# Mask tables from an earlier n, and a softmax normalisation shared by VectorE and GpSimd

## The chip, the cores and the metric

The kernel runs on one core of a Trainium2 chip. The metric is the device time of one execution in microseconds (us). A core has five engines that each run their own list of instructions in order: TensorE (PE, matmuls; its weight loads are listed as PEld), VectorE (DVE), ScalarE (ACT), GpSimd (POOL) and SyncE (SP, which here only issues DMA transfers). An instruction waits on semaphores until what it needs is there, and everything behind it on the same engine waits with it.

## The reference

```python
# q, k, v: (2, 8, 768, 64); n_global = 8, n_local = 96; two MLP layers 512 -> 2048 -> 512
rel = pos[:, None] - pos[None, :]
is_global = pos[None, :] < n_global
is_local = (rel >= 0) & (rel < n_local)
dist = np.where(is_global & ~is_local, n_local, np.abs(rel))
scores = q @ k.T / sqrt(D) - slope[h] * dist          # slope[h] = 2 ** (-8 (h + 1) / H)
scores = np.where(is_global | is_local, scores, -1e9)
a = np.exp(scores - max(scores));  a = a / (sum(a) + 1e-9)
x = (a @ v)            # heads side by side: 1536 tokens x 512
h = x @ w_in;  x = (h * sigmoid(h)) @ w_out           # first layer
h = x @ w2_in; out = np.maximum(0.01 * h, h) @ w2_out  # second layer
```

`n_global` and `n_local` are inputs: they are 64-bit integers that the kernel reads from memory, so the mask is computed on the chip.

## The kernel before

Attention is cut into 24 units (2 batches, 3 blocks of 256 query rows, 4 pairs of heads). Unit n goes through these steps: its q and k arrive by DMA; PE transposes them into the PSUM tile `pt` (L936); ACT or DVE copies them out as `kT` and ACT as `qT`, and DVE repeats the first 32 keys in `kT` (L948); PE computes the scores `s` (L979); DVE adds the mask and takes the row extreme (`nm`, L1012); ACT takes the exponential and its row sum (L1019); DVE makes the reciprocal `rs` of the sums (L1025, L1026) and multiplies the four quarters of the tile `A` by it (L1035, "the normalisation": two row blocks i, two heads j; 256 columns wide, or 128 in the first row block of a sequence); PE transposes `A` into `pa` (L1052, once for each row block, as soon as that block's two quarters are normalised); ACT or DVE copies it to `AT`; PE multiplies by v into `pv` (L1078); ACT and DVE split that into a high and a low part in `x`. There are two buffers of `A`.

The MLP follows: weights arrive as 64-bit numbers in `st`, and ACT and DVE make two 32-bit parts of them (L273 to L288); PE does `ph` and `pq` (first product), `po` (second product). MLP work on PE, DVE and ACT fills the gaps of the attention as far as its inputs are there.

No order is written by hand. `Sched` is a list scheduler that runs while the program is built: every task has engines it may run on, a cost for each, a priority and what it depends on; the scheduler walks through its own modelled time and gives each idle engine the ready task of best priority. What comes out is a fixed list of instructions for each engine. A task with several engines goes to whichever is idle first. Dummy matmuls on zeros (`wps`, L878: 8 at the start, then a few, then 16 as fillers of low priority) keep PE running before there is real work.

At the start q of unit 0, then `n_global` and `n_local`, then q of unit 1 go out on SP's queue, and k of units 0 and 1 on ACT's. The mask (L828 to L844) is made by nine small DVE instructions and two POOL instructions after the two numbers have landed. `mask` serves a full block, `mask0` the first one of a sequence.

DMA transfers of SP and ACT take eight semaphores in turn: the ninth one issued waits until the first has landed.

Of the kernel before, what the change touches and what calls it, by code (L numbers as in the profile page):

```python
# [26 lines left out]
def kernel(  # L27
# [49 lines left out]
    def load_n(eng):  # L77
        for x, src in enumerate((n_global, n_local)):
            eng.dma_start(out=nraw[:, x], in_=src.bitcast(I32).partition_broadcast(P))
# [5 lines left out]
    m8nl = const.tile([P, 1], F32, name="m8nl")  # L85

# [33 lines left out]
    class Sched:  # L120
# [19 lines left out]
        def run(self):  # L140
# [3 lines left out]
            for t in self.tasks:  # L144
                for e in t["eng"]:
                    free.setdefault(e, 0.0)
                    ready.setdefault(e, [])
                for b in t["bufs"]:
                    if b.tile is not None and not b.held:
                        b.held = True  # L150
                        used[b.key] = used.get(b.key, 0) + 1
            seq, dma = 0, 0.0
# [12 lines left out]
            while len(order) < len(self.tasks):  # L165
                for e in free:
# [22 lines left out]
                    if t["dma"]:  # L189
                        dma = max(dma, now + 0.4) + t["land"]  # L190
                        end = max(end, dma) + 1.7
                    else:
                        end += t["land"]
# [591 lines left out]
    with ExitStack() as es:  # L785
# [28 lines left out]
        m8rel, pen, col = mk[:, 0:256], mk[:, 256:512], mk[:, 512:640]  # L814
        nc.gpsimd.iota(
            m8rel[:, P:256], pattern=[[8, P]], base=0, channel_multiplier=-8, allow_small_or_imprecise_dtypes=True
        )
        nc.gpsimd.affine_select(
# [5 lines left out]
        )  # L824
        nc.gpsimd.iota(col, pattern=[[1, P]], base=0, channel_multiplier=0, allow_small_or_imprecise_dtypes=True)

        def masks_n():
            nc.vector.tensor_copy(npair, nraw)  # L828
            nc.vector.tensor_scalar(nhi, npair[:, :, 0], 0.0, None, op0=ALU.is_lt)
            nc.vector.tensor_tensor(nhi, nhi, npair[:, :, 1], op=ALU.add)  # L830
            nc.vector.scalar_tensor_tensor(nf, nhi, float(2.0 ** 32), npair[:, :, 0], op0=ALU.mult, op1=ALU.add)
            nc.vector.tensor_scalar(m8nl, nlf, -8.0, None, op0=ALU.mult)

        def masks_global(eng):
            eng.tensor_scalar(col, col, ngf, -BIG, op0=ALU.is_ge, op1=ALU.mult)
            eng.tensor_scalar(col, col, m8nl, 0.0, op0=ALU.add, op1=ALU.add)

        def masks_local():
            nc.vector.tensor_scalar(pen, m8rel, m8nl, -BIG, op0=ALU.is_le, op1=ALU.mult)
            nc.vector.tensor_tensor(mask, m8rel, pen, op=ALU.add)  # L840

        def masks_both():
            nc.vector.tensor_copy(mask[:, NPV:P], col[:, 0:NG])
            nc.vector.tensor_tensor(mask0, mask[:, P:256], col, op=ALU.max)  # L844

        masks = (masks_n, masks_global, masks_local, masks_both)
# [13 lines left out]
        nload = add("SP", 0.9, lambda eng: load_n(eng), -13.0, (), (), land=0.1)  # L860
        add("ACT", 1.4, lambda eng: eng.activation(warm, warm, AF.Exp), -9.0, (), (), at=2.0)
        mt = add("DVE", 0.95, lambda eng: masks[0](), -0.5, (nload,), (), at=3.9)
        mp = add("POOL", 0.9, lambda eng: masks[1](eng), -0.5, (mt,), ())
        mt = add("DVE", 0.75, lambda eng: masks[2](), -0.5, (mt,), ())
        mtask = add("DVE", 0.45, lambda eng: masks[3](), -0.5, (mt, mp), ())
# [133 lines left out]
        def st_P(u):  # L999
# [30 lines left out]
            for i in range(2):  # L1030
                c0 = P if 2 * sb + i == 0 else 0
                for j in range(2):
                    def norm(eng, i=i, j=j, c0=c0):
                        a = A()[:, i, j, c0:256]
                        eng.tensor_scalar(a, a, rs()[:, 2 * i + j:2 * i + j + 1], None, op0=ALU.mult)  # L1035

                    u["norm"].append(add("DVE", 0.26, norm, n + 0.3, (rt,), (A, rs)))
# [228 lines left out]
```

## Time and profile before

| | |
|---|---|
| time, median of 3 runs | 606.26 us (606.16 to 608.05) |
| time of the profiled execution | 607.96 us |
| span of its instructions | 606.2 us |
| PE busy | 596.1 us (98%) |
| DVE busy | 528.4 us (87%) |
| ACT busy | 305.4 us (50%) |
| POOL busy | 3.7 us (1%) |
| chain that ended last | PE 94%, DVE 3%, DMA 2%, ACT 1% |

The span counts from the first to the last instruction of the trace; 1.8 us lie around it. Busy shares are averages over stages with different limits, so the stages have to be looked at one by one: the start (no input yet), the first units of attention, attention beside the MLP, and the MLP alone.

### The profile page before, as it was taken

To read this page: it belongs to the slowest core of one execution; us is meant where nothing else is said; L and a number is where in the kernel's file an instruction comes from. 1 tells how busy PE (TensorE), PEld (TensorE's weight loads), DVE (VectorE), ACT (ScalarE), POOL (GpSimd) and SP (SyncE) were. 2 spreads that over 40 slices of the span, in tenths; PEclk is the share of its full clock that TensorE was granted. 3 is DMA by queue.
4 is the path that set the end of the run, shared out by engine and by line. 5 is a ranking of instruction groups with operands and counts; after the bars stand their busy time and mean duration, and the time that the engine had idled before them with its cause. 6 is when DMAs were issued, how large, how long until landed. Compare 5 with 4: busy or idle time off the path is not lost.

```text
span 606.2 us, 9115 instructions
## 1 busy us (share of the span) xinstructions
PE 596.1 (98%) x3266; PEld 490.0 (81%) x3267; DVE 528.4 (87%) x1213; ACT 305.4 (50%) x682; POOL 3.7 (1%) x20
## 2 busy tenths in 40 slices
PE   8999999999999999999999999999999999999996
PEld 4678777778888888888888888898898889888985
DVE  4999999877999999995999999899999997978551
ACT  4789887876654435432555554556343433333110
POOL 2000000000000000000000000000000000000000
PEclk9999999999999999999999999999999999999999
DMA  8875568310012332322231111322132322010112
GB/s 180 185 174 141 136 167 203 71 36 1 0 36 70 105 105 69 106 69 70 69 105 35 36 35 36 105 69 85 54 105 71 104 70 69 6 65 1 70 55 90
DMA packets 72676, 49.43 MB, mean 82 GB/s; under 512 B 50480, under 2 KB 67120, under 8 KB 72624
## 3 DMA queue, kind: packets, MB, share of 16 engines
q1 hardware_dynamic: 71536, 48.51, 28.6%
q8 instruction: 28, 0.46, 0.3%
q10 hardware_dynamic: 1088, 0.26, 0.2%
q14 instruction: 24, 0.20, 0.1%
HBM read 45.62 MB, written 3.15 MB: 80 GB/s over the span
## 4 chain that ended last, share of the span: by engine, by line
PE 94%; DVE 3%; DMA 2%; ACT 1%; issue 0%; ACTq 0%
PE po L655 43%; PE pq L490 29%; PE ph L600 10%; PE s L979 3%; PE pa L1052 3%; PE pv L1078 3%; PE pt L936 2%; DMA st<-in_moe_w_in_dram 1%; DVE A L1012 1%; PE wps L878 1%; DMA q<-in_q_dram 1%; DVE A L1035 0%; DMA k<-in_k_dram 0%; ACT AT L222 0%; ACT A L1019 0%; DVE f L279 0%
## 5 line engine op out<-in xcount | busy, mean ns | idle before, releaser
L655 PE MATMUL po<-g,wo 128*128 128x512 f32 x576 | 141.5, 392 | 0.0
L655 PE MATMUL po<-wo,g 128*128 128x512 f32 (+1 forms) x588 | 136.2, 385 | 0.0
L655 PEld LDWEIGHTS po<-wo,g 128*128 128x128 f32 x588 | 107.7, 188 | 21.0
L655 PEld LDWEIGHTS po<-g,wo 128*128 128x128 f32 x576 | 106.9, 188 | 21.7 <-DVE wo L288 0.2
L600 PE MATMUL ph<-x,wi 128*128 128x512 f32 (+1 forms) x336 | 77.6, 366 | 0.9 <-DVE wi L288 0.6
L505 DVE TENSOR_TENSOR tl<-tl,pq 128x512 f32<-128x512 f32 (+1 forms) x110 | 64.3, 585 | 10.3 <-PE pq L490 5.3
L600 PEld LDWEIGHTS ph<-x,wi 128*128 128x128 f32 x336 | 56.4, 188 | 11.0 <-DVE wi L288 1.2
L490 PE MATMUL pq<-xs,ws 128*128 128x512 f32 x252 | 62.3, 389 | 0.0
L490 PEld LDWEIGHTS pq<-xs,ws 128*128 128x128 f32 x252 | 47.3, 188 | 9.8
L273 ACT ACTIVATE st<-st 128x512 f32<-128x512 f32 x64 | 42.9, 670 | 23.5 <-DMA st<-in_moe_w_out_dram 13.2
L1019 ACT ACTIVATE A<-A,nm 128x256 f32<-128x256 f32 (+1 forms) x96 | 46.1, 483 | 12.1 <-DVE nm L1012 11.9
L687 DVE SCALAR_TENSOR_TENSOR yp<-po,yp 128x512 f32<-128x512 f32 x60 | 40.7, 686 | 9.4 <-PE po L655 9.1
L279 DVE SCALAR_TENSOR_TENSOR f<-st,f 128x512 int32<-128x512 int32 x64 | 43.9, 687 | 0.9
L282 DVE SCALAR_TENSOR_TENSOR f<-st,f 128x512 int32<-128x512 int32 x64 | 43.8, 684 | 0.4
L575 ACT ACTIVATE g<-tl 128x512 fp32r<-128x512 f32 x40 | 25.0, 630 | 37.5 <-DVE tl L570 29.0
L490 PE MATMUL pq<-xn,wi 128*128 128x512 f32 (+1 forms) x192 | 43.1, 336 | 0.0
L1012 DVE CUSTOM_DVE_ANT_0 A<-s,mask 128x256 f32<-128x256 f32 (+1 forms) x96 | 34.7, 393 | 3.9 <-PE s L979 3.7
L222 ACT ACTIVATE wo<-f 128x512 fp32r<-128x512 f32 x30 | 18.9, 630 | 34.6 <-PE po L655 17.2
L490 PEld LDWEIGHTS pq<-xn,wi 128*128 128x128 f32 x192 | 32.3, 189 | 4.5
L578 DVE TENSOR_TENSOR g<-tl,g 128x512 fp32r<-128x512 f32 x40 | 27.1, 686 | 5.1 <-ACT g L575 4.8
L575 ACT ACTIVATE g<-t 128x512 fp32r<-128x512 f32 x32 | 20.1, 630 | 19.7 <-PE po L655 10.8
L276 DVE TENSOR_SCALAR f<-st 128x512 int32<-128x512 int32 x64 | 26.7, 420 | 1.6 <-ACT st L273 1.6
(119 smaller groups left out, 883.2 us busy)
## 6 DMA issues: line engine op xcount, KB each, us to landing
st<-in_moe_w_in_dram SPq DMA_DIRECT2D x32, 512.0 KB, 3.8
st<-in_moe_w_out_dram SPq DMA_DIRECT2D x32, 512.0 KB, 3.6
vd<-in_v_dram SPq DMA_DIRECT2D x24, 128.0 KB, 2.8
q<-in_q_dram SPq DMA_DIRECT2D x22, 128.0 KB, 3.1
k<-in_k_dram SPq DMA_DIRECT2D x22, 128.0 KB, 3.4
out_dram<-yo SPq DMA_DIRECT2D x11, 256.0 KB, 2.1
vp<-in_v_dram SPq DMA_DIRECT2D x20, 96.0 KB, 2.7
vp<-in_v_dram SPq DMA_DIRECT2D x20, 32.0 KB, 2.4
```

The costliest lines, as they stand in the source:

```text
L273: eng.activation(hf, hf, AF.Copy, scale=2.0 ** -112)
L279: eng.scalar_tensor_tensor(fi(), lo(), 29, fi(), op0=ALU.logical_shift_right, op1=ALU.bitwise_or)
L282: eng.scalar_tensor_tensor(fi(), hi(), -(2 ** 31), fi(), op0=ALU.bitwise_and, op1=ALU.bitwise_or)
L490: eng.matmul(bank[c]()[:, :w], wt_()[:, a, f0:f0 + P], x()[:, b, c0:c0 + w], start=(first and kk == 0 and i == 0), stop=(kk == 1 and i == ...
L505: eng.tensor_tensor(dst[0]()[:, dst[1]], a[0]()[:, a[1]], b[0]()[:, b[1]], op=op)
L575: eng.activation(g()[:, 0, :], t(), AF.Copy)
L578: eng.tensor_tensor(g()[:, 1, :], t(), g()[:, 0, :].bitcast(F32), op=ALU.subtract)
L600: eng.matmul(ph()[:, :w], wv[:, a, kk, :], xs[kk]()[:, b, cs], start=(kk == 0 and i == 0), stop=(kk == NKK - 1 and i == 2),)
L655: eng.matmul(po()[:, :w], lhsT, rhs, start=(j == 0 and i == 0), stop=(j == FPP - 1 and i == 2))
L687: eng.scalar_tensor_tensor(dst()[:, cs], po()[:, :w], scale, y()[:, cs], op0=ALU.mult, op1=ALU.add)
L1012: eng.tensor_tensor_reduce(A()[:, i, j, c0:256], s[j]()[:, i, c0:256], mask0 if c0 else mask, -QSCALE * SLOPE[2 * hp + j], 3.0e38, ALU.add ...
L1019: eng.activation(a, a, AF.Exp, bias=nm()[:, x:x + 1], scale=-1.0, accum_out=su()[:, x:x + 1])
```

## The change

Five things change.

1. `n_global` goes out first on ACT's queue and `n_local` first on SP's, ahead of q and k.
2. POOL prepares tables without knowing n: `far` (where `pen` was) and `col` hold numbers on a scale of 2^41 whose sign flips at the limit once 2^42 n is added. When n is there, DVE makes the local mask in one instruction (`far` plus `nfar`, minimum with `m8rel`) and the global one in three. The two POOL instructions that came after n are gone; three come before it.
3. The normalisation task may run on DVE (cost 0.3) or POOL (cost 0.65). Before, it was DVE only (cost 0.26).
4. The scheduler's model of time: SP and ACT are free from 0.75, and a DMA task ends no earlier than 2.4 after its issue.
5. Priorities and costs of the tasks for n and the mask.

```diff
-    def load_n(eng):
-        for x, src in enumerate((n_global, n_local)):
-            eng.dma_start(out=nraw[:, x], in_=src.bitcast(I32).partition_broadcast(P))
+    def load_n(eng, x):
+        eng.dma_start(out=nraw[:, x], in_=(n_global, n_local)[x].bitcast(I32).partition_broadcast(P))
...
-                    free.setdefault(e, 0.0)
+                    free.setdefault(e, 0.75 if e in ("SP", "ACT") else 0.0)
...
-                        end = max(end, dma) + 1.7
+                        end = max(end + 2.4, dma + 1.7)
...
-        m8rel, pen, col = mk[:, 0:256], mk[:, 256:512], mk[:, 512:640]
+        m8rel, far, col = mk[:, 0:256], mk[:, 256:512], mk[:, 512:640]
...
+        nc.gpsimd.tensor_scalar(far[:, P:256], m8rel[:, P:256], BIG / 4, -BIG, op0=ALU.mult, op1=ALU.add)
...
+        nc.gpsimd.tensor_scalar(far[:, 0:P], m8rel[:, 0:P], BIG / 4, -BIG, op0=ALU.mult, op1=ALU.add)
         nc.gpsimd.iota(col, pattern=[[1, P]], base=0, channel_multiplier=0, allow_small_or_imprecise_dtypes=True)
+        nc.gpsimd.tensor_scalar(col, col, -2 * BIG, -BIG, op0=ALU.mult, op1=ALU.add)
...
-            nc.vector.tensor_scalar(nhi, npair[:, :, 0], 0.0, None, op0=ALU.is_lt)
-            nc.vector.tensor_tensor(nhi, nhi, npair[:, :, 1], op=ALU.add)
+            nc.vector.scalar_tensor_tensor(nhi, npair[:, :, 0], 0.0, npair[:, :, 1], op0=ALU.is_lt, op1=ALU.add)
             nc.vector.scalar_tensor_tensor(nf, nhi, float(2.0 ** 32), npair[:, :, 0], op0=ALU.mult, op1=ALU.add)
             nc.vector.tensor_scalar(m8nl, nlf, -8.0, None, op0=ALU.mult)
-
-        def masks_global(eng):
-            eng.tensor_scalar(col, col, ngf, -BIG, op0=ALU.is_ge, op1=ALU.mult)
-            eng.tensor_scalar(col, col, m8nl, 0.0, op0=ALU.add, op1=ALU.add)
+            nc.vector.tensor_scalar(nfar, nf, 2 * BIG, None, op0=ALU.mult)
 
         def masks_local():
-            nc.vector.tensor_scalar(pen, m8rel, m8nl, -BIG, op0=ALU.is_le, op1=ALU.mult)
-            nc.vector.tensor_tensor(mask, m8rel, pen, op=ALU.add)
-
-        def masks_both():
+            nc.vector.scalar_tensor_tensor(mask, far, nfar[:, 1:2], m8rel, op0=ALU.add, op1=ALU.min)
+
+        def masks_global():
+            nc.vector.tensor_scalar(col, col, nfar[:, 0:1], m8nl, op0=ALU.add, op1=ALU.min)
+            nc.vector.tensor_tensor(mask0, mask[:, P:256], col, op=ALU.max)
             nc.vector.tensor_copy(mask[:, NPV:P], col[:, 0:NG])
-            nc.vector.tensor_tensor(mask0, mask[:, P:256], col, op=ALU.max)
...
-        nload = add("SP", 0.9, lambda eng: load_n(eng), -13.0, (), (), land=0.1)
-        add("ACT", 1.4, lambda eng: eng.activation(warm, warm, AF.Exp), -9.0, (), (), at=2.0)
-        mt = add("DVE", 0.95, lambda eng: masks[0](), -0.5, (nload,), (), at=3.9)
...
+        nload = [
+            add(e, 0.42, lambda eng, x=x: load_n(eng, x), -15.0, (), (), land=0.05, dma=True)
+            for x, e in enumerate(("ACT", "SP"))
+        ]
+        add("ACT", 1.4, lambda eng: eng.activation(warm, warm, AF.Exp), -9.0, (), (), at=2.7)
+        mt = add("DVE", 1.0, lambda eng: masks_n(), -5.0, nload)
+        mt = add("DVE", 0.43, lambda eng: masks_local(), -2.0, (mt,))
+        mtask = add("DVE", 0.6, lambda eng: masks_global(), -2.0, (mt,))
...
-                        eng.tensor_scalar(a, a, rs()[:, 2 * i + j:2 * i + j + 1], None, op0=ALU.mult)
-
-                    u["norm"].append(add("DVE", 0.26, norm, n + 0.3, (rt,), (A, rs)))
+                        r = rs()[:, 2 * i + j:2 * i + j + 1]
+                        if eng is nc.gpsimd:
+                            eng.tensor_scalar(a, a, r, 1.0, op0=ALU.mult, op1=ALU.mult)
+                        else:
+                            eng.tensor_scalar(a, a, r, None, op0=ALU.mult)
+
+                    u["norm"].append(add(("DVE", "POOL"), (0.3, 0.65), norm, n + 0.3, (rt,), (A, rs)))
```

Since the scheduler decides, the lists of all engines move. Three places are shown. The first is PE's list at the start, from the transposes of unit 1 on (`pt`: transposes of q and k, `wps`: dummy matmuls, `s_198` and `s_200`: scores of unit 0). Before:

```order
L936 MATMUL pt<-ident,q 128x128 x2
L936 MATMUL pt<-ident,k 128x128 x2
L878 LDWEIGHTS zero
L878 MATMUL wps<-zero 128x512
L878 LDWEIGHTS zero
L878 MATMUL wps<-zero 128x512
L878 LDWEIGHTS zero
L878 MATMUL wps<-zero 128x512
L979 MATMUL s_198<-kT,qT 128x128
L979 MATMUL s_200<-kT,qT 128x128
L979 MATMUL s_198<-kT,qT 128x256
L979 MATMUL s_200<-kT,qT 128x256
```

Now, from the transposes of unit 0 on (the scores of unit 0 are `s_195` and `s_197`):

```order
L938 MATMUL pt<-ident,q 128x128 x2
L938 MATMUL pt<-ident,k 128x128 x2
L880 LDWEIGHTS zero
L880 MATMUL wps<-zero 128x512
L880 LDWEIGHTS zero
L880 MATMUL wps<-zero 128x512
L938 MATMUL pt<-ident,q 128x128 x2
L938 MATMUL pt<-ident,k 128x128 x2
L981 MATMUL s_195<-kT,qT 128x128
L981 MATMUL s_197<-kT,qT 128x128
L981 MATMUL s_195<-kT,qT 128x256
L981 MATMUL s_197<-kT,qT 128x256
```

Three dummies stood between the transposes of unit 1 and the scores of unit 0; now two stand ahead of those transposes, and nothing behind them. Behind the scores of unit 0 comes one dummy, then the scores of unit 1 and the transposes of unit 2, and then 9 dummies where there were 10.

The second place is DVE's list at the start, from the landing of n to the first masked scores (`npair`, `nhi`, `nf`, `m8nl`, `nfar`: n as floats, `mk`: the tables, `kT`: the repeated keys). Before:

```order
L828 CAST npair<-nraw 128x4
L829 TENSOR_SCALAR nhi<-npair 128x2
L830 TENSOR_TENSOR nhi<-nhi,npair 128x2
L831 SCALAR_TENSOR_TENSOR nf<-nhi,npair 128x2
L832 TENSOR_SCALAR m8nl<-nf 128x1
L839 TENSOR_SCALAR mk<-mk,m8nl 128x256
L840 TENSOR_TENSOR mask<-mk 128x256
L948 COPY kT<-kT 128x5x32
L843 COPY mask<-mk 128x32
L844 TENSOR_TENSOR mask_119<-mask,mk 128x128
L948 COPY kT<-kT 128x5x32
L1012 ISA A,nm<-s_198,mask_119 128x128
```

Now:

```order
L834 CAST npair<-nraw 128x4
L835 SCALAR_TENSOR_TENSOR nhi<-npair 128x2
L836 SCALAR_TENSOR_TENSOR nf<-nhi,npair 128x2
L837 TENSOR_SCALAR m8nl<-nf 128x1
L838 TENSOR_SCALAR nfar<-nf 128x2
L841 SCALAR_TENSOR_TENSOR mask<-mk,nfar 128x256
L844 TENSOR_SCALAR mk<-mk,nfar,m8nl 128x128
L845 TENSOR_TENSOR mask_120<-mask,mk 128x128
L846 COPY mask<-mk 128x32
L950 COPY kT<-kT 128x5x32 x2
L1014 ISA A,nm<-s_195,mask_120 128x128
```

All of the mask now stands ahead of both copies of the repeated keys, and no DVE instruction in between waits for POOL's work after n.

The third place is the normalisation of unit 4, on DVE before (`A_436` is its tile, `rs_521` its reciprocals):

```order
L1025 TENSOR_SCALAR rs_521<-su_444 128x4
L1026 RECIPROCAL rs_521<-rs_521 128x4
L282 SCALAR_TENSOR_TENSOR f_503<-st_279,f_503 128x512
L1035 TENSOR_SCALAR A_436<-A_436,rs_521 128x256 x4
L1093 TENSOR_TENSOR x_538<-pv_512,x_538 128x256
L288 TENSOR_TENSOR wi_543<-f_503,wi_543 128x512
```

Now on DVE (`A_492` and `rs_540`):

```order
L1027 TENSOR_SCALAR rs_540<-su_502 128x4
L1028 RECIPROCAL rs_540<-rs_540 128x4
L1099 TENSOR_TENSOR x_535<-pv_507,x_535 128x256
L1041 TENSOR_SCALAR A_492<-A_492,rs_540 128x256 x2
L283 SCALAR_TENSOR_TENSOR f_514<-st_287,f_514 128x512
```

and on POOL, units 0 to 5:

```order
L1039 TENSOR_SCALAR A_207<-A_207,rs_250 128x128
L1039 TENSOR_SCALAR A_207<-A_207,rs_250 128x256
L1039 TENSOR_SCALAR A_234<-A_234,rs_289 128x128
L1039 TENSOR_SCALAR A_308<-A_308,rs_365 128x128
L1039 TENSOR_SCALAR A_379<-A_379,rs_443 128x128
L1039 TENSOR_SCALAR A_379<-A_379,rs_443 128x256
L1039 TENSOR_SCALAR A_492<-A_492,rs_540 128x256 x2
L1039 TENSOR_SCALAR A_517<-A_517,rs_628 128x256 x2
```

Of the 96 normalisations 45 move to POOL, in most units the first and the last of four, so each row block of `A` waits for one quarter from each engine. PE's transposes `pa` of unit 4 wait for POOL at their first and for POOL again at their last quarter.

## Rows read from the trace of the kernel before

**Rows 1.** Windows: us, then PE, PEld, DVE, ACT, POOL busy us, granted clock

```profile
13.70:43.48 29.78, 27.68 (x240) 20.81 (x240) 28.59 (x118) 24.88 (x81) 0.00 (x0) 1.00 0.79 189
43.48:143.00 99.52, 99.24 (x794) 77.83 (x796) 89.19 (x327) 80.12 (x243) 0.00 (x0) 1.00 0.47 118
```

**Rows 2.** Chain that ended last, 13.70 to 43.48, its shares by line

```profile
by line: DMA st<-in_moe_w_in_dram 17.5%; DVE A L1012 12.6%; PE pa L1052 8.2%; DVE A L1035 7.4%; ACT AT L222 7.4%; ACT A L1019 5.4%; DVE wi L288 4.3%; PE s L979 4.0%; issue 3.4%; PE pv L1078 2.7%; DVE rs L1026 2.4%; DVE AT L224 2.3%; DVE x L
```

**Rows 3.** The same chain piece by piece at the start: start us, us, what

```profile
6.35 1.22 PE pt L936 x4
7.56 1.28 PE wps L878 x3
8.84 2.24 PE s L979 x16
11.08 0.59 PE pt L936 x4
11.67 2.16 PE wps L878 x10
13.83 0.34 PE pa L1052 x2
```

**Rows 4.** Timeline, start: start us, us, engine, line, what [idle <-releaser]

```profile
0.73 2.06 ACTq L893 DMA_DIRECT2D k<-in_k_dram  x4
...
1.21 3.60 PE L878 MATMUL wps<-zero 128*128 128x512 bf16 x8 [1.21 <-DVE zero L868]
...
2.24 0.43 SPq L79 DMA_DIRECT2D nraw<-in_n_local_dram  x1
...
2.82 1.28 ACT L861 ACT_TABLE_LOAD   x1 [2.82 <-issue]
...
4.60 0.64 PE L936 MATMUL pt<-ident,q 128*128 128x128 f32 x2
```

**Rows 5.** DMA issues before 14 us: count, KB, us to landing

```profile
k<-in_k_dram ACTq DMA_DIRECT2D x4, 64.0 KB, 2.7
...
nraw<-in_n_global_dram SPq DMA_DIRECT2D x1, 1.0 KB, 2.7
```

**Rows 6.** Timeline of the start, DVE and POOL: the mask

```profile
2.90 0.24 POOL L825 IOTA mk<- 128x128 f32 x1
...
5.80 0.17 DVE L828 CAST npair<-nraw 128x4 f32<-128x4 int32 x1 [4.64 <-DMA nraw<-in_n_local_dram]
...
6.75 0.73 POOL L835 TENSOR_SCALAR mk<-mk,nf 128x128 f32<-128x128 f32 x1 [3.61 <-DVE m8nl L832]
6.86 0.41 DVE L839 TENSOR_SCALAR mk<-mk,m8nl 128x256 f32<-128x256 f32 x1
...
7.58 0.80 POOL L836 TENSOR_SCALAR mk<-mk,m8nl 128x128 f32<-128x128 f32 x1
...
8.40 0.18 DVE L843 COPY mask<-mk 128x32 f32<-128x32 f32 x1 [0.51 <-POOL mk L836]
...
10.46 0.29 DVE L1012 CUSTOM_DVE_ANT_0 A<-s,mask 128x128 f32<-128x128 f32 x1 [1.51 <-PE s L979]
```

**Rows 7.** Groups of POOL by shape: busy us, mean ns of one

```profile
L818 POOL TENSOR_SCALAR_AFFINE_SELECT mk<-mk 128x128 f32<-128x128 f32 x1 | 0.3, 295 | 0.0
```

**Rows 8.** Timeline, units 4, 8 and 23: reciprocal, normalisation, transposes of A

```profile
30.14 0.18 DVE L1026 RECIPROCAL rs<-rs 128x4 f32<-128x4 f32 x1
...
30.81 1.13 DVE L1035 TENSOR_SCALAR A<-A,rs 128x256 f32<-128x256 f32 x4
...
55.26 0.18 DVE L1026 RECIPROCAL rs<-rs 128x4 f32<-128x4 f32 x1
...
56.15 1.29 PE L1052 MATMUL pa<-ident,A 128*128 128x128 f32 x8
...
139.12 0.18 DVE L1026 RECIPROCAL rs<-rs 128x4 f32<-128x4 f32 x1
...
139.96 1.09 PE L1052 MATMUL pa<-ident,A 128*128 128x128 f32 x8
```

More of the change, by code (lines that the diff above doesn't have):

```diff
@@ L85 @@
     m8nl = const.tile([P, 1], F32, name="m8nl")
+    nfar = const.tile([P, 2], F32, name="nfar")
     qsc = const.tile([P, NHP], F32, name="qsc")
@@ L151, in run @@
                         used[b.key] = used.get(b.key, 0) + 1
-            seq, dma = 0, 0.0
+            dma = 0.0
+            heapq.heappush(ev, (0.75, -1, 2))
             def enter(t):
@@ L824 @@
         )
+        nc.gpsimd.tensor_scalar(far[:, 0:P], m8rel[:, 0:P], BIG / 4, -BIG, op0=ALU.mult, op1=ALU.add)
         nc.gpsimd.iota(col, pattern=[[1, P]], base=0, channel_multiplier=0, allow_small_or_imprecise_dtypes=True)
+        nc.gpsimd.tensor_scalar(col, col, -2 * BIG, -BIG, op0=ALU.mult, op1=ALU.add)
         def masks_n():
             nc.vector.tensor_copy(npair, nraw)
-            nc.vector.tensor_scalar(nhi, npair[:, :, 0], 0.0, None, op0=ALU.is_lt)
-            nc.vector.tensor_tensor(nhi, nhi, npair[:, :, 1], op=ALU.add)
+            nc.vector.scalar_tensor_tensor(nhi, npair[:, :, 0], 0.0, npair[:, :, 1], op0=ALU.is_lt, op1=ALU.add)
             nc.vector.scalar_tensor_tensor(nf, nhi, float(2.0 ** 32), npair[:, :, 0], op0=ALU.mult, op1=ALU.add)
             nc.vector.tensor_scalar(m8nl, nlf, -8.0, None, op0=ALU.mult)
-        def masks_global(eng):
-            eng.tensor_scalar(col, col, ngf, -BIG, op0=ALU.is_ge, op1=ALU.mult)
-            eng.tensor_scalar(col, col, m8nl, 0.0, op0=ALU.add, op1=ALU.add)
+            nc.vector.tensor_scalar(nfar, nf, 2 * BIG, None, op0=ALU.mult)
         def masks_local():
-            nc.vector.tensor_scalar(pen, m8rel, m8nl, -BIG, op0=ALU.is_le, op1=ALU.mult)
-            nc.vector.tensor_tensor(mask, m8rel, pen, op=ALU.add)
-        def masks_both():
+            nc.vector.scalar_tensor_tensor(mask, far, nfar[:, 1:2], m8rel, op0=ALU.add, op1=ALU.min)
+        def masks_global():
+            nc.vector.tensor_scalar(col, col, nfar[:, 0:1], m8nl, op0=ALU.add, op1=ALU.min)
+            nc.vector.tensor_tensor(mask0, mask[:, P:256], col, op=ALU.max)
             nc.vector.tensor_copy(mask[:, NPV:P], col[:, 0:NG])
-            nc.vector.tensor_tensor(mask0, mask[:, P:256], col, op=ALU.max)
-        masks = (masks_n, masks_global, masks_local, masks_both)
         sc = Sched(dict(SIZES, pt=2, s=4, q=2, k=2, vd=2, vp=2, nm=4, su=4, rs=4))
@@ L858 @@
         kT, kdone = {}, {}
-        nload = add("SP", 0.9, lambda eng: load_n(eng), -13.0, (), (), land=0.1)
-        add("ACT", 1.4, lambda eng: eng.activation(warm, warm, AF.Exp), -9.0, (), (), at=2.0)
-        mt = add("DVE", 0.95, lambda eng: masks[0](), -0.5, (nload,), (), at=3.9)
-        mp = add("POOL", 0.9, lambda eng: masks[1](eng), -0.5, (mt,), ())
-        mt = add("DVE", 0.75, lambda eng: masks[2](), -0.5, (mt,), ())
-        mtask = add("DVE", 0.45, lambda eng: masks[3](), -0.5, (mt, mp), ())
+        nload = [
[6 more added lines that the diff above has]
+        mtask = add("DVE", 0.6, lambda eng: masks_global(), -2.0, (mt,))
         add("DVE", 0.6, lambda eng: flags(), 20.0, (mtask,), at=20.0)
```

## The prediction

> **What bounds the kernel now.** I read four views, in this order: the busy times in stretches, the chain of waits, the timeline of the first 14 us, and the groups by shape.
>
> The stretches split the span in three. From 43.48 to 143.00, where attention runs beside the MLP, PE is busy 99.24 of 99.52 us, while DVE is busy 89.19 and ACT 80.12 [rows 1]. PE is the bound there, and what a faster DVE gives back is not worth a microsecond unless PE would have waited. Behind 143 there is MLP work only, which the change doesn't touch. Time can come from the first 43 us alone, and it can be lost anywhere before 143.
>
> From 13.70 to 43.48 DVE is busy 28.59 of 29.78 us and ACT 24.88 [rows 1]. The chain goes through DVE, ACT, PE and a weight transfer by turns; the normalisation (`DVE A L1035`) has 7.4% of that stretch, 2.2 us [rows 2].
>
> At the start the chain is PE's own list: transposes of unit 1, three dummies (1.28 us), the scores of units 0 and 1, transposes of unit 2, ten dummies (2.16 us), the first `pa` at 13.83 [rows 3]. A dummy takes 0.45 us in the first eight (3.60 us) and 0.216 in the ten [rows 3, 4]: the same 512 columns at the lower of TensorE's two levels (1.2 GHz) first and at the higher one (2.4) later, after PE has run almost without a break since 1.21. From 13.70 on the granted clock is 1.00 [rows 1]. The mask is not what the first masked scores wait for: DVE's last mask wait ends at 8.40 and DVE then stands idle for 1.51 us until `s` comes at 10.46 [rows 6].
>
> **Start: n first, mask, dummies.** n lands earlier. `n_local` was issued at 2.24 and the cast that needs it started at 5.80 [rows 4, 6]; now both numbers are issued at 0.73, where k's first was [rows 4], and land 2.7 us later as `n_global` did [rows 5], at 3.4. POOL's three added table instructions cost 0.73 to 0.80 each if they are like the two that go [rows 6], so the tables that were ready at 3.14 (2.90 + 0.24) are ready by 5.5. DVE needs about 1 us of small instructions after n, then three for the masks: ready near 6.2, instead of after 8.4. By itself that is worth nothing, as the 1.51 us of idle time shows. Its worth is that DVE copies the repeated keys right after, and that the scheduler, which knows it, puts the scores of unit 0 directly behind the transposes of unit 1.
>
> The price: q and k of unit 0 are issued one transfer later, 0.43 on SP, and k 0.5 (2.06 for four) on ACT [rows 4]. k's second half then goes out at 1.7 and lands at 4.4 [rows 5]; PE is in its eight dummies until 4.8 and its first transposes start at 4.60 [rows 4], so this is covered by 0.2 us; without that cover the whole start moves by up to 0.3. k's fourth transfer has to wait for a semaphore until `n_global` has landed, at 3.4, and lands at 6.1, when the transposes of unit 1 were due anyway (6.35) [rows 3]. ACT's table load (1.28) stands behind it, so it ends at 5.2 instead of 4.1 [rows 4], with the first copy of `kT` due at 5.7.
>
> Now PE's list: transposes of unit 0 from 4.60 for at most 1.22 [rows 3, 4], two dummies at 0.45, so 6.7; transposes of unit 1 (1.22) to 7.9; there the scores of unit 0 start, against 8.84. Then 2.24 for both scores, one dummy between them (0.22 to 0.45, take 0.3), 0.59, and nine dummies at 0.216 (1.94): the first `pa` at 13.0 against 13.83 [rows 3]. I take -0.9, with ends of -1.4 (the dummies at the higher level, as the first `pa` could then come when its quarters are ready) and +0.5 (the transfers late, the level rising later).
>
> **The normalisation, 13.7 to 43.5.** 45 of 96 quarters go to POOL, 12 of the 28 of units 0 to 6, which lie in this stretch. On DVE four wide ones take 1.13 us, 0.28 each [rows 8]. Counted on the chain alone, 12 of 28 of 2.2 us is 0.9; if all twelve stood in the way of something, 3.4. ACT, idle for 4.9 us in the stretch [rows 1], would not stop that. I take -1.2, nearer to the chain's figure, since PE, ACT and a transfer hold more of that chain than DVE's normalisation.
>
> **What a POOL quarter costs.** No row shows it. Below it is bounded by POOL's plainest pass over 128 columns, 0.295 us [rows 7]; above by twice the dearer of the two scalar instructions, 1.6 for 256 columns [rows 6]. Those two took 0.73 and 0.80 with DVE at work beside them. DVE fell idle at 7.89 (8.40 less 0.51) and POOL ended at 8.38, so 0.49 is the least that the second one needed by itself [rows 6]. I take 0.5 for 128 columns and 0.75 for 256, between that and the 0.80. Both ends stay in the range.
>
> **What waits for it.** With a hop of 0.1, POOL's second quarter is done 1.6 us after the reciprocal, where DVE alone finished four 1.6 us after it, an `f` instruction between them included (30.32 to 31.94) [rows 8]. In the DVE-bound stretch that is a draw. Behind 43.48 every late `pa` stops a full PE. Before, `pa` began 0.71 us after the reciprocal in unit 8 and 0.66 in unit 23 [rows 8]; these are the first and the last of the four such gaps below 1 us in units 7 to 23 (0.71, 0.44, 0.90, 0.66; the next two are 1.04 and 1.09). The second row block comes some 0.5 later, half a `pa`, so unit 8 would be late by 1.6 - 1.2 = 0.4; over the four and the next that makes 1.75 us. Against it, DVE has 0.56 us less to do in each unit, and with DVE busy 90% there [rows 1] its reciprocals come earlier by up to that: 0.1 is left. I take +0.1, with 1.75 as the upper end.
>
> **Sum.** -0.9 - 1.2 + 0.1 = -2.0. The profiled execution took 607.96 (span 606.2, 1.8 around it), so it would take 606.0; it lies 1.7 above the median of 606.26, which is what I forecast from: 604.3 us. About 0.3%, 1.8 us, is what a measurement of this kernel can tell from no change, so the forecast sits just beyond that line.
>
> **Rivals.**
> *DVE was the whole bound* (chance 0.15). If all twelve quarters pay and POOL needs no more than 0.5: -0.9 - 3.4 + 0 gives 602.0. For it: 28.59 of 29.78. Against: the chain's 17.5% for a weight transfer and the shares of PE and ACT [rows 2].
>
> *It cancels out* (0.22). The earlier scores are paid back because DVE, not PE's list, releases the second and third unit, and the relief on DVE sits beside other waits: -0.3, 606.0. For it: from 13.83 on the chain soon leaves PE [rows 2, 3]. Against: DVE's list is shorter too.
>
> *POOL and DVE get in each other's way* (0.18), the case on the slower side. DVE starts its two quarters as the reciprocal ends and POOL's first comes through only behind them (0.56), then needs its own 0.5, and the second 0.75 more: 1.9 us after the reciprocal, and more when the next DVE instruction gets in between, say 2.3 (1.1 a quarter). Late `pa`s then: 2.3 less 0.56 of relief, 0.5 for the second block and the gap, which is 0.5 in unit 8 and 2.6 over the six tightest; in the first stretch half of 0.7 in each of six units, 2.1. With the start that is -0.9 + 2.6 + 2.1 = +3.8 if no relief is left, and +2.6 if the 1.2 is: 608.9. It decides from about 0.9 a quarter on, where the same sum is nought. For it: 0.73 and 0.80 for half the columns. Against: in the one place where both ran, DVE's table instruction took 0.41 us and ended 0.2 before POOL's did, though POOL had started first [rows 6], so DVE at least was not held up.
>
> The Trainium skill has a rule that would make this rival the rule (SBUF — State Buffer, "Who interferes with whom"): the two engines share a pair of ports as an exclusive lock, and a DVE `tensor_scalar` from SBUF to SBUF, or one with two SBUF inputs, shuts out a GpSimd instruction, or is shut out by it, until the first is through. By that rule the row has POOL waiting rather than DVE, which no row excludes.
>
> **How the numbers follow.** The forecast has 0.45, its own range 603.2 to 605.4. For 8 in 10 I go from 601.8 to 608.7: it leaves out the far half of the first rival and the upper half of the third, and holds the bounds of the start (-1.4, +0.5) and of the relief. Faster by over 0.3% (below 604.4): the forecast's better part (0.27), the first rival (0.15), a little of the second: 0.45. Within: 0.37. Slower (above 608.1): the third rival, 0.18.
>
> **What would show it.** Right: the cast of n near 3.5; the scores of unit 0 near 7.9; the first `pa` near 13.0; PE saturated about 2 us earlier than 43.5; a POOL quarter of 0.75. Wrong: PE waits before `pa` for POOL behind 43 us; POOL quarters near 1.1; DVE's `f` and normalisation instructions longer than before; a first transpose later than 4.9.

## The result and the profile after

The changed kernel takes 611.12 us (median of 6 runs, 609.16 to 611.82), the kernel before beside it 606.21: ratio 1.0075, 95% interval 1.0061 to 1.0089. It is slower by 4.9 us, where 604.3 was forecast. Its profiled execution took 611.28 us with a span of 609.5.

One thing has to be known before the two traces are compared. The kernel before was profiled a second time (`b1` below), in an execution of 606.21. The list of instructions and the transfers at the start are the same, but TensorE reaches the higher of its two clock levels earlier, during the first transposes at 4.60. PE's list in that second profile, timeline (start us, us, engine, line, what):

```profile
7.07 0.81 PE L878 MATMUL wps<-zero 128*128 128x512 bf16 x3
7.81 1.92 PE L979 MATMUL s<-kT,qT 64*128 64x128 f32 x16
...
12.31 0.38 PE L1052 MATMUL pa<-ident,A 128*128 128x128 f32 x2
```

In the timeline of the first profile the three dummies took 1.49 us instead of 0.81, the scores 2.31 instead of 1.92, and the first `pa` came at 13.73 (the chain of [rows 3] counts from 13.83). The column of the granted clock reads 1.00 in both, so the level is to be read from such durations. So the executions of one kernel differ by 1.4 us at the first `pa`, and by 1.8 us at the last output instruction (below), with the same instructions in the same order. Both profiles of the changed kernel reached the higher level late. Against the first profile of before, which did too, the changed kernel's last output instruction is 3.0 us later (603.37 against 600.38). The rest of the 4.9 would be that the runs of before lie mostly in their lower group (near 606.1, the other near 607.5). Whether the change made the late rise more frequent stays open: in the table of runs below, 5 of the 9 profiles of kernels that send n first show it, and 1 of the 10 others, which is too few to settle it.

The stretches of the changed kernel (us, then PE, PEld, DVE, ACT, POOL busy, granted clock, DMA share, GB/s):

```profile
13.70:43.48 29.78, 26.78 (x235) 20.02 (x235) 27.07 (x108) 24.39 (x81) 5.97 (x10) 1.00 0.76 189
43.48:60.00 16.52, 14.65 (x132) 12.58 (x131) 16.08 (x49) 12.73 (x38) 2.53 (x6) 1.00 0.56 147
60.00:143.00 83.00, 82.94 (x652) 63.13 (x652) 72.46 (x251) 64.87 (x198) 16.43 (x29) 1.00 0.47 115
```

and the second profile of before:

```profile
13.70:43.48 29.78, 27.69 (x247) 21.41 (x246) 29.23 (x119) 25.29 (x82) 0.00 (x0) 1.00 0.83 199
43.48:60.00 16.52, 16.51 (x152) 13.88 (x151) 16.27 (x57) 15.15 (x45) 0.00 (x0) 1.00 0.48 130
60.00:143.00 83.00, 82.72 (x640) 63.54 (x639) 71.98 (x268) 63.77 (x194) 0.00 (x0) 1.00 0.46 112
```

PE was full from 43.48 before [rows 1]; now it is full only from 60 and has 0.9 us less to show in the first stretch and 1.9 in the second. DVE is hardly freer there: 10 of its quarters are gone in the first stretch, yet it is busy 27.07 of 29.78. Behind 60 nothing is lost. The loss lies between 13.7 and 60. PE's longest waits there are 1.08 us at 26.50 for a quarter from POOL and this one, for DVE's half of the split of `pv`:

```profile
58.98 1.06 PE L1058 MATMUL pa<-ident,A 128*128 128x128 f32 x8 [1.36 <-DVE x L1099]
```

Neither profile of before lists a wait for `x`.

The start, chain of the changed kernel (start us, us, what), which answers to [rows 3]:

```profile
1.18 3.98 DMA q<-in_q_dram
5.16 0.14 issue
5.30 1.28 PE pt L938 x4
6.58 0.85 PE wps L880 x2
7.43 0.85 PE pt L938 x4
8.29 1.58 PE s L981 x8
9.87 0.54 PE wps L880
10.41 0.88 PE s L981 x8
11.29 0.59 PE pt L938 x4
11.88 1.94 PE wps L880 x9
13.82 0.22 PE pa L1058 x2
```

The scores start 0.55 us earlier, as meant, but `pa` comes at 13.82 against 13.83: q now holds the chain until 5.16, and the two scores with their dummy take 3.0 us. From the timeline and the list of transfers of the changed kernel, against [rows 4, 5]:

```profile
4.83 0.17 DVE L834 CAST npair<-nraw 128x4 f32<-128x4 int32 x1 [3.66 <-DMA nraw<-in_n_global_dram]
...
5.23 1.28 ACT L864 ACT_TABLE_LOAD   x1 [5.23 <-DMA nraw<-in_n_global_dram]
5.30 0.85 PE L938 MATMUL pt<-ident,q 128*128 128x128 f32 x2 [0.49 <-DMA q<-in_q_dram]
...
9.90 0.29 DVE L1014 CUSTOM_DVE_ANT_0 A<-s,mask 128x128 f32<-128x128 f32 x1 [0.91 <-PE s L981]
...
11.80 0.51 SPq L265 DMA_DIRECT2D st<-in_moe_w_in_dram  x1
```

```profile
k<-in_k_dram ACTq DMA_DIRECT2D x4, 64.0 KB, 4.2
q<-in_q_dram SPq DMA_DIRECT2D x4, 64.0 KB, 4.0
...
nraw<-in_n_global_dram ACTq DMA_DIRECT2D x1, 1.0 KB, 4.1
```

`n_global` goes out 1 us earlier and lands in 4.1 us instead of 2.7; the first q and k, now behind n, need 4.0 and 4.2, where they needed 2.7. The mask is ready near 6.9, the masked scores wait for `s` as before. The last row, the first weight load at 11.80, is taken up below.

The normalisation, groups of the changed kernel (busy us, mean ns of one | idle before), against [rows 7, 8]:

```profile
L1039 POOL TENSOR_SCALAR A<-A,rs 128x256 f32<-128x256 f32 x37 | 22.1, 606 | 74.3 <-DVE rs L1028 29.9 <-PE pv L1084 12.0 <-ACT x L1096 11.0
L819 POOL TENSOR_SCALAR mk<-mk 128x128 f32<-128x128 f32 x1 | 0.3, 302 | 0.0
...
L1041 DVE TENSOR_SCALAR A<-A,rs 128x256 f32<-128x256 f32 x43 | 19.2, 481 | 0.1
```

and units 4 and 6 in its timeline:

```profile
31.25 0.18 DVE L1028 RECIPROCAL rs<-rs 128x4 f32<-128x4 f32 x1
...
31.62 1.64 POOL L1039 TENSOR_SCALAR A<-A,rs 128x256 f32<-128x256 f32 x2 [4.58 <-ACT kT L223]
31.65 0.75 DVE L1041 TENSOR_SCALAR A<-A,rs 128x256 f32<-128x256 f32 x2
...
43.10 0.96 POOL L1039 TENSOR_SCALAR A<-A,rs 128x256 f32<-128x256 f32 x2 [3.58 <-PE pt L938]
43.14 1.07 DVE L1041 TENSOR_SCALAR A<-A,rs 128x256 f32<-128x256 f32 x2
```

In unit 6 two quarters on each engine, begun together, take 1.1 us; four on DVE alone took 1.13 [rows 8]. In unit 4, where DVE goes on to an `f` instruction, POOL's pair takes 1.64. DVE's own wide quarter went from 347 ns (the group's mean in both profiles of before) to 481. The three table instructions took 0.30 us each, where 0.73 to 0.80 had been assumed; nothing waited for them.

### The profile page after: what moved, and what is told of

Same layout as the page of the kernel before. It is cut to its first block, busy times and chain, and to the rows that moved or that the text cites. A ratio compares the mean times of both kernels' runs of the same rounds, so it can differ in the third digit from the quotient of the medians.

```text
span 609.5 us, 9186 instructions
## 1 busy us (share of the span) xinstructions
PE 596.7 (98%) x3267; PEld 489.4 (80%) x3267; DVE 525.5 (86%) x1172; ACT 304.6 (50%) x678; POOL 28.7 (5%) x66
## 4 chain that ended last, share of the span: by engine, by line
PE 92%; DVE 5%; ACT 1%; DMA 1%; POOL 0%; issue 0%; SPq 0%; POOLq 0%; DVEq 0%
PE po L656 43%; PE pq L491 29%; PE ph L601 9%; PE s L981 3%; PE pa L1058 3%; PE pv L1084 3%; PE pt L938 2%; DVE A L1014 1%; PE wps L880 1%; DVE A L1041 1%; DMA q<-in_q_dram 1%; ACT A L1021 1%; POOL A L1039 0%; DVE f L280 0%; DVE AT L225 0%
## 5 line engine op out<-in xcount | busy, mean ns | idle before, releaser
L1039 POOL TENSOR_SCALAR A<-A,rs 128x256 f32<-128x256 f32 (+1 forms) x45 | 25.7, 581 | 110.5 <-DVE rs L1028 43.5
```

## The experiments

All numbers of the runs in one table: median, first `pa`, PE busy from 13.70 to 60.00, and the start of the last output instruction (`yo`, L687 in the kernel before), the last three from the profiled execution. An early first `pa` (12.2 to 12.4) is the early rise of TensorE's clock, 13.2 to 13.7 the late one. A profile is best compared with one of the same kind: an early one with b1, a late one with the first profile of before. The medians mix both kinds. z1's profile is of its fastest run, 606.61.

| run | what | us | first `pa` | PE busy | last `yo` |
|---|---|---|---|---|---|
| before, first profile | | 606.2 | 13.73 | 44.20 | 600.38 |
| b1 | before, second profile | 606.2 | 12.31 | 44.20 | 598.54 |
| s1 | new tables, n second, old order | 606.13 | 12.18 | 44.30 | 598.55 |
| x3 | new order (0.28) | 606.74 | 12.31 | 43.74 | 598.88 |
| z3 | new order (exponential) | 606.88 | 12.35 | 42.90 | 599.38 |
| s2 | s1 with n first, old order | 607.27 | 12.23 | 42.98 | 599.82 |
| x1 | shared, old order | 607.60 | 12.30 | 43.39 | 600.09 |
| z2 | new order (0.30) | 608.31 | 12.27 | 42.23 | 600.79 |
| z1 | new order (0.24) | 608.35 | 12.31 | 43.46 | 599.57 |
| e4 | start alone | 608.89 | 12.40 | 42.61 | 601.20 |
| e3 | model of time alone | 609.03 | 12.43 | 42.17 | 601.15 |
| y1 | e1, new order (0.28) | 609.18 | 13.56 | 42.43 | 601.84 |
| e2 | sharing alone | 609.34 | 12.30 | 41.44 | 601.72 |
| e1 | start and model | 609.37 | 12.31 | 42.37 | 601.42 |
| k1 | whole change, old order | 609.44 | 13.52 | 42.79 | 602.17 |
| y2 | change with other costs | 610.82 | 12.38 | 41.62 | 602.39 |
| a1 | the change again | 610.89 | 13.17 | 41.37 | 602.99 |
| after | the change, first profile | 611.12 | 13.66 | 41.43 | 603.37 |
| x2 | the change's order, all on DVE | 613.17 | 13.17 | 40.76 | 603.40 |

**The parts, each planned anew.** e1 takes the changed kernel and puts the normalisation back on DVE; e2, e3 and e4 put one part each into the kernel before. Only the lines that matter are shown, here and in the cuts below.

```diff
 e1, e4:  the task of n, tables, mask (e4 with the old model of time)
 e2
-  add("DVE", 0.26, norm, ...)
+  add(("DVE", "POOL"), (0.3, 0.65), norm, ...)
 e3
-  end = max(end, dma) + 1.7
+  end = max(end + 2.4, dma + 1.7)
```

> The whole change but for the normalisation, which stays on DVE alone (cost 0.26). Theory S (the loss comes from sharing the normalisation: a quarter on POOL and a quarter on DVE beside each other take as long as two on DVE, so DVE gets no relief, while the plan was made as if it did): 605 to 607, within 1 us of before. Theory N (the loss comes from the start: n goes out ahead of q and k, so the first transposes and ACT's table load are 0.7 to 2.4 us later): 609 to 611, as the whole change. Theory P (any new plan of this scheduler moves the time by several us either way): no number, but e1, e2, e3 and e4 then don't add up to the whole.

> The kernel before with the normalisation on DVE or POOL and nothing else of the change. Theory S: 609 to 611.5. Theory N: 605 to 607. In both, two POOL quarters beside two DVE quarters take about 1.0 us, as they did with the whole change.

> The kernel before with the scheduler's model alone changed (SP and ACT free from 0.75, a DMA no shorter than 2.4). No instruction is added or removed, only the order. Theories S and N: 605 to 607.5. Theory P: this alone moves the time by more than 2 us.

> The kernel before with n first on two queues, the mask from tables, and their priorities and costs; the scheduler's model and the normalisation as before. Theory S: 605 to 607, the scores of unit 0 earlier but the first transposes later. Theory N: 608 to 611, since the late landing of q is in this part.

Ratios 1.0050 (1.0032 to 1.0067), 1.0047 (1.0030 to 1.0064), 1.0038 (1.0024 to 1.0052) and 1.0047 (1.0029 to 1.0066): each part alone costs 2.4 to 2.8 us, and start and model together no more than either. e3 adds no instruction and takes none away. So neither the sharing nor the start alone is the cause, and a new order is suspected.

**What a new order costs by itself.** One cost in the plan of the kernel before is changed, nothing else.

```diff
 x3, z1, z2
-  add("DVE", 0.26, norm, ...)
+  add("DVE", 0.28, norm, ...)          # 0.24 in z1, 0.30 in z2
 z3
-  add("ACT", 0.42 if c0 else 0.51, exp, ...)
+  add("ACT", 0.43 if c0 else 0.52, exp, ...)
 y1: e1 with 0.28 instead of 0.26
```

> The kernel before with one number of the scheduler's model changed: a normalisation costs 0.28 there instead of 0.26. No instruction is added, removed or given to GpSimd; only the order changes, in the middle of the attention and not at the start. Theory P (the order of the kernel before is a favourable one, and nearly any new order loses 2 to 3 us): 608 to 609.5. Theories L and R, which put the loss on the sharing or on the start: 605.5 to 606.8.

> The kernel before, a normalisation at 0.24 in the plan instead of 0.26, no instruction changed. If new orders differ by 2 to 3 us among themselves and that of the kernel before is among the better ones: anywhere from 606 to 609.5. If new orders cost nothing, as 0.28 did: 605.8 to 606.8.

> The kernel before, a normalisation at 0.30 in the plan instead of 0.26, no instruction changed. Orders that differ: 606 to 609.5. Orders that cost nothing: 605.8 to 606.8.

> The kernel before, an exponential at 0.52 (0.43 for the narrow one) in the plan instead of 0.51 (0.42), no instruction changed. Orders that differ: 606 to 609.5. Orders that cost nothing: 605.8 to 606.8.

> The new start and the new model of time without the sharing, as in the run that took 609.37, with one number changed: a normalisation costs 0.28 in the plan instead of 0.26, so the order of the middle is another and the start the same. If the loss of that run was only an unlucky order: 606 to 607.5. If the new start or the new model costs 2 to 3 us whatever the order behind it: 608.5 to 610.

Against before on the same chip: 1.0004 (0.9994 to 1.0014), 1.0031 (1.0019 to 1.0043), 1.0034 (1.0019 to 1.0049), 1.0016 (1.0005 to 1.0027). Orders that differ by nothing that anyone meant are 0.4 to 1.9 us slower by their medians, and none of the four is faster than the old one. By the last `yo`, all four with the early rise, they lie 0.3 to 2.3 us behind b1; e3 and e4 lie 2.6 and 2.7 behind it. e4 and y1 (1.0037) have n first as well, which costs something by itself (below). For e3 an order a little worse than z2's would be enough, so nothing beyond its order is shown to cost time in it.

**n first.** s1 has the new tables and the mask as one minimum, but n behind the first q. The lists of PE, ACT and SP come out the same as in the kernel before, instruction by instruction. s2 keeps these lists and only issues n first.

```diff
 s2 against s1
+  nc.scalar.dma_start(n_global), nc.sync.dma_start(n_local)   # ahead of the first task
-  add("SP", 0.9, lambda eng: load_n(eng), -13.0, ...)
+  add("SP", 0.9, lambda eng: None, -13.0, ...)
```

> The kernel before with the new tables and the mask as one minimum, but with n behind the first q as before, the old model of time, no sharing. If the loss of the start (608.89 against 606.53) is the transfer of n ahead of q and k: 605.8 to 607. If it is the new order that follows from new tasks at the start: 608 to 609.5.

> The run with the new tables and n behind q, which took 606.13, with n_global issued first on ScalarE's queue and n_local first on SyncE's, ahead of q and k. The order of everything else on every engine stays as in the kernel before. If n ahead of q and k costs the 2.5 us by itself (first transposes 0.7 late, the table load 2.4 late): 608 to 609. If the cost comes with the new order that the scheduler makes of it: 605.8 to 606.8.

s1 equals before (1.0000, 0.9990 to 1.0010): the tables cost nothing, and the 0.1 us by which `pa` comes earlier is not seen in the time. s2 loses 1.1 us against s1 (against before 1.0017, 1.0007 to 1.0027, or 1.0 us). Where, the timelines show; s1:

```profile
10.69 0.51 SPq L265 DMA_DIRECT2D st<-in_moe_w_in_dram  x1
...
15.68 0.70 ACT L274 ACTIVATE st<-st 128x512 f32<-128x512 f32 x1 [1.95 <-DMA st<-in_moe_w_in_dram]
...
17.70 1.30 PE L978 MATMUL s<-kT,qT 64*128 64x128 f32 x8 [0.45 <-ACT qT L950]
```

s2:

```profile
11.80 0.51 SPq L266 DMA_DIRECT2D st<-in_moe_w_in_dram  x1
...
17.06 0.65 ACT L275 ACTIVATE st<-st 128x512 f32<-128x512 f32 x1 [3.39 <-DMA st<-in_moe_w_in_dram]
...
18.78 0.49 PE L979 MATMUL s<-kT,qT 64*128 64x128 f32 x4 [1.53 <-ACT qT L951]
```

Up to the first `pa` both run alike (12.18 and 12.23). But `n_global`, q and k take 1.3 to 1.5 us longer to land, and the transfers behind them take the eight semaphores in turn: SP stands 1.9 us until `n_local` has landed, and the first weight load is issued 1.1 us later. ACT's first work on the weights stands ahead of a `qT` on its list, waits 3.39 us instead of 1.95, and PE waits 1.08 us longer for `qT`. In every kernel with n first this load is issued at 11.80 to 11.88, in every other at 10.63 to 10.69. So the late load belongs to the change of queue order, not to a plan. What it costs depends on the rest. In k1 below, which has the old order and the late rise, ACT waits 2.62 us for it and PE 0.65 for that `qT`, 0.2 more than in the first profile of before (0.45). In the changed kernel ACT begins on the weights only at 19.98 and doesn't wait for the load at all.

**The sharing.** x1 keeps the old order and issues the first and last quarter of each unit on POOL; x2 keeps the order of the changed kernel and issues all on DVE; y2 gives the scheduler costs nearer to what was measured.

```diff
 x1, in norm
+  if i != j: eng.tensor_scalar(...)
+  else: nc.gpsimd.tensor_scalar(...)
 x2, in norm
-  if eng is nc.gpsimd: ...
+  nc.vector.tensor_scalar(a, a, r, None, op0=ALU.mult)
 y2
-  add(("DVE", "POOL"), (0.3, 0.65), norm, ...)
+  add(("DVE", "POOL"), (0.45, 0.55), norm, ...)
```

> The kernel before with its scheduler's order kept as it is; only the first and the last of each unit's four normalisations are issued on GpSimd instead of VectorE, at the same place of the order (48 of 96). No new plan, so this shows what the sharing does by itself. Theory L (the two engines shut each other out, four quarters take about 1.0 us on both against 1.13 on VectorE alone, so nothing is relieved, and the pair ends late when another VectorE instruction gets in between): 606.5 to 609. Theory R (the relief of VectorE is real and the loss of the changed kernel comes from elsewhere): 604.5 to 605.5. Theory P (a new plan is what costs, the sharing costs nothing to speak of): 605.5 to 607.

> The changed kernel with its scheduler's order kept, but every normalisation issued on VectorE, also the 45 that were planned for GpSimd. Theory L: four quarters take 1.13 us instead of 1.0, and none is held up by other VectorE work: 609.5 to 611.5, so no slower than the changed kernel. Theory R: VectorE loses 0.56 us of relief in each of the units that it bounds: 612 to 614. Theory P: the order is what costs, so the same as the changed kernel within 1 us: 610 to 612.

> The changed kernel with other costs for the normalisation in the plan: 0.45 on VectorE and 0.55 on GpSimd instead of 0.3 and 0.65, near what they take beside each other. The scheduler then gives GpSimd fewer of them (16 of 96) and VectorE fewer other copies. If the last 2 us of the loss come from a plan that believes VectorE relieved: 608.5 to 610. If they come from the sharing itself, by the share of quarters that stays: 609.5 to 611. If any order with sharing loses them: 611.

x1 loses 1.3 us (1.0022, 1.0011 to 1.0034), with 48 quarters on POOL and the order unchanged. DVE's busy time from 13.70 to 143 falls from 117.49 (b1) to 112.47: 5.0 us for 48 quarters, 0.10 each (over the whole span 528.38 to 523.84, 0.09 each). Against that, what PE waits for in that stretch (us in total, times, longest), in b1:

```profile
PE pa L1052 <- DVE A L1035: 1.0, 2, 0.7
PE ph L600 <- DVE wi L288: 0.6, 1, 0.6
```

and in x1:

```profile
PE pa L1056 <- POOL A L1039: 1.5, 3, 0.9
PE ph L600 <- DVE wi L288: 0.8, 1, 0.8
PE pa L1056 <- DVE x L1097: 0.6, 2, 0.3
```

The waits for a normalised `A` grow by 0.5 us, those for `x` by 0.6 and those for `wi` by 0.2; PE's busy time in the stretch falls by 1.3 (126.92 to 125.59), which is the loss. Nowhere does the relief of DVE reach PE.

x2 took 613.17, but its last `yo` starts within 0.03 us of the changed kernel's (603.40 and 603.37): the difference in its profile lies behind the last output, where 7.0 us pass instead of 5.7. So its time says nothing on the sharing. Counted from the first `pa` to the last `yo`, x2 takes 590.23 us, the changed kernel 589.71 and a1 589.82: in that order the sharing costs nothing and may gain 0.4 to 0.5, by three profiles. PE's long wait for `x` is there without any sharing, so it is the order's:

```profile
59.34 1.06 PE L1055 MATMUL pa<-ident,A 128*128 128x128 f32 x8 [1.40 <-DVE x L1096]
```

y2 stays at 610.82 (1.0076). Its expectation counted 16 quarters on POOL, but its profile shows 51 (43 wide and 8 narrow), more than the 45 of the changed kernel. So it doesn't show what fewer shared quarters do; it shows that these costs in the plan don't bring the time back.

**What the two engines do to each other.** m1 leaves attention and MLP out. It runs eight DVE instructions of a kind alone, then beside eight POOL normalisations.

```diff
+ for parts in ((dve,), (gps,), (dve, gps), (act,), (act, gps), (two,), (two, gps), (psum,), (psum, gps)):
+     for i in range(8):
+         for f in parts: f(i)
```

> Not the reference's computation: attention and MLP are left out and the output is filled with zeros. It runs eight instructions of a kind by themselves and then beside eight GpSimd normalisations of 128x256, each engine on its own tiles. Theory L: VectorE's normalisation 0.28 us alone and GpSimd's 0.45 to 0.5 alone; beside each other the sum of both, 0.75 a pair, not the larger; the same with VectorE instructions that have two SBUF inputs; no lengthening beside ScalarE. Theory R: 0.5 a pair, the larger of the two, and VectorE's at 0.28 to 0.3 still.

Its timeline: DVE alone, POOL alone, both together; then with a DVE instruction of two SBUF inputs, alone and together; then a DVE copy from PSUM, alone and together.

```profile
7.55 2.18 DVE L81 TENSOR_SCALAR dt<-dt,r 128x256 f32<-128x256 f32 x8
...
10.60 3.65 POOL L84 TENSOR_SCALAR pt<-pt,r 128x256 f32<-128x256 f32 x8 [10.16 <-DVE r L78]
...
14.94 3.43 DVE L81 TENSOR_SCALAR dt<-dt,r 128x256 f32<-128x256 f32 x8
15.20 3.96 POOL L84 TENSOR_SCALAR pt<-pt,r 128x256 f32<-128x256 f32 x8 [0.94 <-DVE r L78]
...
28.40 6.25 DVE L90 SCALAR_TENSOR_TENSOR y<-w,r,x 128x512 f32<-128x512 f32 x8
...
35.34 6.92 DVE L90 SCALAR_TENSOR_TENSOR y<-w,r,x 128x512 f32<-128x512 f32 x8
35.59 7.02 POOL L84 TENSOR_SCALAR pt<-pt,r 128x256 f32<-128x256 f32 x8 [7.94 <-DVE r L78]
...
43.30 2.73 DVE L93 COPY dt<-pp 128x256 f32<-128x256 f32 x8
...
46.71 2.73 DVE L93 COPY dt<-pp 128x256 f32<-128x256 f32 x8
46.96 3.65 POOL L84 TENSOR_SCALAR pt<-pt,r 128x256 f32<-128x256 f32 x8 [4.35 <-DVE r L78]
```

A DVE quarter takes 0.27 us alone and 0.43 beside POOL, a POOL quarter 0.46 alone and 0.50 beside DVE: sixteen quarters are done in 4.2 us on both engines, and would take 4.4 on DVE alone. Beside an instruction like `f` a POOL quarter takes 0.88, one for each DVE instruction, which it lengthens by 0.08. Beside a copy from PSUM neither slows. So theory L's sum of both (0.75 a pair) is wrong, and so is theory R's unhindered DVE. Beside ScalarE's copies POOL's eight took 3.65 us as well, as alone.

**The whole change in the old order.** k1 is s2 with the quarters of x1; b1 and a1 are before and after once more.

> The kernel before once more, unchanged, for a second profile: its executions fall in two groups, near 606.1 and near 607.6, and the one profiled so far took 607.96. If what differs lies behind the last output instruction (code and output transfers), the last yo ends at 600.8 again; if it lies in the attention, the last yo ends near 599.3 in an execution of 606.1, and the first 60 us show where.

> All of the change in the old order: new tables, n first on two queues, the first and the last normalisation of each unit on GpSimd, and the order of every engine as in the kernel before. If n first (1.1) and the sharing (1.3) add and the rest of the loss is the new order: 608 to 609, and the changed kernel beside it 2 to 3 slower. If the parts together cause the loss whatever the order: 610.5 to 611.5.

> The changed kernel once more, unchanged, on the chip of the run with the old order: 610.5 to 611.5. If its executions fall in two groups by when TensorE's clock rises at the start, as those of the kernel before do (near 606.1 and 607.6), the lower group is near 609.2.

k1 takes 609.44 (1.0048, 1.0031 to 1.0065), a1 beside it 610.89 (1.0080, 1.0063 to 1.0097), before 606.35. By the medians k1 loses 3.1 and the new order 1.5 more, from four runs each. But k1's profile has the late rise, where most runs of before don't seem to, so that 3.1 is not only its parts. Among the late profiles the last `yo` starts at 600.38 before, 602.17 in k1, 602.99 in a1 and 603.37 in the changed kernel's first profile: 1.8 us for n first and the sharing in the old order, 0.8 to 1.2 more for the new order. No version beat the kernel before; s1 equals it.

## Why the prediction was wrong

*What bounds the kernel* held for the kernel before: PE full behind the first stretch, DVE busy nearly all of it, the mask not waited for. That time given back to DVE shortens that stretch did not show: from 13.70 to 43.48 DVE is busy 27.90 us in x1 and 29.23 in b1, and PE gets through 27.49 against 27.69.

*The start, -0.9.* It was 0.0 at the first `pa`, and behind it up to +1.1 (s2). The step that failed first is "both numbers ... land 2.7 us later": the duration came from a transfer issued behind q, and it took 4.1 ahead of it, and with it went q (first transposes at 5.30, not 4.60), the table load (ended at 6.5, not 5.2) and the scores (8.29, not 7.9). Another step was left out: the prediction followed q, k and n through the ring of semaphores, and not the first weight load further down SP's queue. PE waited 1.1 us longer behind it in s2 and 0.2 in k1; in the changed kernel's own order no wait for it is seen.

*The relief, -1.2.* A quarter moved to POOL was priced as 0.28 us of DVE given back. It gives back 0.10 in the kernel and (4.36 - 3.43)/8 = 0.12 in m1. With the same share of the chain, that makes -0.4, and even that was not seen in the old order: PE waited longer in x1, not less.

*Late `pa`s, +0.1.* In x1 PE waited 1.5 us for POOL in three places, 0.5 more than for DVE's quarters before, and 0.8 more for `x` and `wi`, which the prediction did not follow. Relief and late `pa`s together were to be -1.1; in the old order they are +1.3. In the changed kernel PE waits for POOL at 26.50 and 27.09 (1.2 us), not behind 43, though in x1 one wait of 0.5 lies at 85.9.

*POOL's quarter, 0.75.* 0.61 in the kernel, 0.46 alone, 0.88 beside an instruction like `f`: inside the bounds. Of the prediction's signs of being wrong, the late first transpose (5.30) and the longer normalisations on DVE came, a POOL quarter near 1.1 and waits for POOL behind 43 us did not in the changed kernel.

*The rivals.* "POOL and DVE get in each other's way" came nearest, at 608.9, and had the mechanism of the missing relief; its chance of 0.18 was too low. Its sizes were not right: a quarter of 1.1 was measured at 0.61, below the 0.9 from which it was to decide, and it kept the -0.9 of the start and had no new order. Its objection, that DVE was not held up in the one place where both ran, was read from one instruction. The Trainium skill (SBUF — State Buffer, "Who interferes with whom") speaks of an exclusive lock under which the second engine fully blocks. That the engines contend, m1 shows; that one blocks the other fully, it doesn't: 0.50 for a pair of normalisations, where one after the other would be 0.27 + 0.46 = 0.73, and 0.88 for a pair with a two-input instruction, where it would be 0.78 + 0.46 = 1.24. By the Trainium skill's rule in the same section for a DVE instruction with one SBUF input at most, a copy from PSUM leaves POOL alone, and the trace agrees (0.46 and 0.34, as alone).

*What no step had.* The new order itself. The sum took every instruction that moves at its old value and the rest of the plan as equal; four orders that differ by one cost lost 0.4 to 1.9 us, and this one 0.8 to 1.2 against k1 by the last `yo`. Its long wait for `x` at 59 us is one place where that time goes. The base was off as well: the first profile was corrected by 1.7 to the median, and 1.4 of that lies ahead of the first `pa`, where dummies and scores ran at the lower level. The gain was worked out from those rows, so part of it is one that an execution of 606.2 has already.

So of the 4.9 us, 2.6 to 3.0 are seen between profiles of the same kind: a start that gained nothing, a sharing that gave DVE little, and an order that made PE wait. How they share it depends on the order, as x1 and x2 show, and how much of the other 2 us is the later rise of the clock stays open.

## What to carry to other kernels

Work that moves from VectorE to GpSimd between SBUF tiles gives back what a run of both engines side by side shows, here 0.10 to 0.12 us of 0.28, and its result comes later. A transfer put ahead of a queue can delay everything that takes its semaphores in turn (here the first weight load by 1.1 us), so follow the queue to the first load that an in-order engine waits for. Where a list scheduler fixes the order, first measure what a meaningless change of its costs does, and judge an edit in a kept order before judging it in a new one. Count in the trace what the plan really moved, and compare profiles in which the clock rose at the same place.

## What was not expected of the hardware

- Two numbers of 1 KB each ahead of q and k slow both. Before, the first q and k opened the queues and landed in 2.2 and 2.4 us (the first of each; 2.7 is the median of four), and `n_global` behind q took 2.7. With n ahead, the two numbers took 4.1 and 3.8 us, and q and k 4.0 and 4.2. Before, the transfers moved 37 GB/s between 1.5 and 2.0 us; with n ahead, at most 1 GB/s up to 3.0. Why is not shown.
- TensorE reaches its higher level at different places of the same instruction list from one execution to the next; the last output instruction of the kernel before moved from 598.54 to 600.38 with it.
- From the end of the last output instruction to the end of the span, 7.0 us passed in x2 and 5.7 in the changed kernel, whose PE lists are the same; in x2 the queues that carry instructions moved 9 packets behind 599 us, in the other 6.
